# Six-step F(3,3) groups beside F(2,3) groups in a dilated convolution with a tanh-sigmoid gate

## The chip, the cores and the metric

The kernel runs on one core of a Trainium2 chip. The metric is the device time of one execution in microseconds (us). The profile is one execution of the program on the chip, taken by the hardware profiler. Its engines are called TensorE (PE in the rows, PEld for its weight loads), VectorE (DVE), ScalarE (ACT), GpSimd (POOL) and SyncE (SP, the queue from which most DMAs are issued).

## What is computed

Two sequences of 16000 steps with 256 channels (bf16) go through a causal convolution with three taps and dilation 2, to 512 channels. The first 256 channels pass through tanh, the other 256 through a sigmoid, the two are multiplied, and the product is multiplied by a 256x256 matrix.

```python
B, T, D, K = (2, 16000, 256, 3)
xp = jnp.pad(x, ((0, 0), (4, 0), (0, 0)))
h = jnp.einsum('btc,cd->btd', xp[:, 4:4 + T, :], w[0])
for i in range(1, K):
    off = 4 - 2 * i
    h = h + jnp.einsum('btc,cd->btd', xp[:, off:off + T, :], w[i])
f, g = h[..., :D], h[..., D:]
out = (jnp.tanh(f) * sigmoid(g)) @ w_o
```

So h[t] = x[t] w0 + x[t-2] w1 + x[t-4] w2. Steps of one parity form a chain of their own, and a short-filter (Winograd) scheme can be used on it: F(2,3) makes two successive outputs of a chain from four products instead of six, F(3,3) three from five instead of nine. The price is sums: of inputs and of weights ahead of the products, and of products behind them.

## The kernel before, in words

**Tiling.** The steps are cut into rows of four. A group is 256 rows (1024 steps; the first and the last group have 160), and a column of a matmul is one row and one parity, 512 columns in all. A transposed DMA (`load_chunk`, L115) brings x with channels on partitions; two groups share a load. For each group VectorE makes the sums `mm` (L185) and `pp` (L191), and GpSimd the four pieces of the differences `dd` (L202). A piece on GpSimd is made to wait for the VectorE instruction named `last`, so that it runs while VectorE's combine reads PSUM.

**Blocks.** A group has four blocks, one for each 128 of the 512 output channels, and the main loop runs over blocks `k`. A block has four products of two matmuls each (`products`, L226). Product 2 goes into bank `b`, ScalarE copies it (`ss`, L257), product 1 is added to `b`, VectorE makes `a = -2 ss + b` (L265), and products 0 and 3 are added to `b` and `a`. ScalarE then applies tanh or sigmoid to both banks (L281). In slot `k` of the loop TensorE does product 2 of block k, product 1 of block k-1, products 0 and 3 of block k-2, and one output piece.

**Output.** `gate` (L290) multiplies tanh and sigmoid halves. `out_mm` (L301) multiplies 128 rows and two steps by `w_o`, `out_evict` (L315) has ScalarE copy the piece to `osb`, and a DMA on SP stores it (L318). A 256-row group has four pieces.

**Start.** The first group (160 rows) is brought in plainly, transposed on TensorE and computed directly with nine products' worth of matmuls (`direct`, L246), while VectorE makes the weight sums `wm` and `wp` (L151 to L154). `direct` accumulates into bank `a` behind a VectorE memset (L243).

All work is issued by hand in program order (a manual schedule): each engine takes its instructions in that order, and waits come from the data and from buffers that must come free (three each of the banks `a` and `b`, two for output pieces).

Of the kernel before, what the change touches and what calls it, by code (L numbers as in the profile page):

```python
# [13 lines left out]
def kernel(  # L14
# [10 lines left out]

# [12 lines left out]
    P = 128  # L38
# [8 lines left out]
    FIRST = (160,)  # L47
    TILES = ((0, 80), (80, 80))
    N_DIRECT = 4

    def sizes(first):
        rem, rs = T // 4, []
        for r in first:
            r = min(r, rem)
            if r > 0:
                rs.append(r)
                rem -= r
        while rem > 0:
            rs.append(min(RG, rem))
            rem -= rs[-1]  # L60
        return rs


    groups, chunks = [], []
    for b in range(B):
        r0 = 0
        rs = sizes(FIRST if b == 0 else ())
        cuts = [1, 1] if b == 0 else []
        i = 0
        while i < len(rs):  # L70
# [33 lines left out]
    xts = {}  # L104

    def load_chunk(c):
        b, r0, rc, _, _ = chunks[c]
        xt = xt_pool.tile([P, 4, CT, RH + XW], bf16, name="xt")
        xts[c] = xt
        if r0 == 0:  # L110
            nc.gpsimd.memset(xt[:, :, :, RH - 1:RH], 0.0)
        if c == 0:
            return
        lo = 0 if r0 == 0 else RH
        nc.sync.dma_start_transpose(  # L115
            out=xt[:, :, :, RH - lo:RH + rc].rearrange("p j ct r -> p (j ct) r"),
            in_=x[b, 4 * (r0 - lo):4 * (r0 + rc), :].rearrange("(r j) c -> r (j c)", j=4),
        )

# [18 lines left out]
    nc.sync.dma_start(out=wo_sb[:], in_=w_o.rearrange("(ct c) d -> c ct d", c=P))  # L138
    ident = consts.tile([P, P], bf16)
    make_identity(nc, ident[:])  # L140
    for c in range(3):
        load_chunk(c)
    loaded = 3

    wh_sb = consts.tile([P, CT, D2], bf16)
    wt_sb = consts.tile([P, CT, D2], f32)
    wp_sb = consts.tile([P, CT, D2], bf16)
    wm_sb = consts.tile([P, CT, D2], bf16)

    def weights():  # L150
        nc.vector.tensor_scalar_mul(wh_sb[:], w_taps[1], 0.5)  # L151
        nc.vector.tensor_tensor(out=wt_sb[:], in0=w_taps[0][:], in1=w_taps[2], op=ALU.add)  # L152
        for dst, op in ((wm_sb, ALU.subtract), (wp_sb, ALU.add)):
            nc.vector.scalar_tensor_tensor(  # L154
                out=dst[:], in0=wt_sb[:], scalar=0.5, in1=wh_sb[:], op0=ALU.mult, op1=op,
            )

    def turn(i):
        r0, r = TILES[i]
        for h in range(2):  # L160
# [8 lines left out]
            dst = xts[0][:, 2 * h:2 * h + 2, :, RH + r0:RH + r0 + r]  # L169
# [5 lines left out]
    def views(g):  # L175
        G = groups[g]
        xt, c, R = xts[G["chunk"]], RH + G["col"], G["R"]
        return (xt[:, 0:2, :, c - 1:c - 1 + R], xt[:, 2:4, :, c - 1:c - 1 + R],
                xt[:, 0:2, :, c:c + R], xt[:, 2:4, :, c:c + R])

    def pre_m(g):
        xp, yp, xc, yc = views(g)
        G = groups[g]
        G["m"] = m_pool.tile([P, 2, CT, RG], bf16, name="mm")
        return nc.vector.tensor_tensor(out=G["m"][:, :, :, :G["R"]], in0=xc, in1=yp, op=ALU.subtract)  # L185

    def pre_p(g):
        xp, yp, xc, yc = views(g)
        G = groups[g]
        G["p"] = p_pool.tile([P, 2, CT, RG], bf16, name="pp")  # L190
        return nc.vector.tensor_tensor(out=G["p"][:, :, :, :G["R"]], in0=xc, in1=yp, op=ALU.add)  # L191

    def pre_d(g, part, eng, behind=None):
        xp, yp, xc, yc = views(g)
        G = groups[g]
        R = G["R"]
        if "d" not in G:
            G["d"] = d_pool.tile([P, 4, CT, RG], bf16, name="dd")
        h, q = divmod(part, 2)
        a, s = (yc, yp) if h == 0 else (xp, xc)  # L200
        j = 2 + q if h == 0 else q
        ins = eng.tensor_tensor(out=G["d"][:, j, :, :R], in0=a[:, q], in1=s[:, q], op=ALU.subtract)  # L202
        if behind is not None:
# [4 lines left out]
            )  # L208

    def products(k, which):  # L210
        g, oi = divmod(k, 4)
        G = groups[g]
        o = O_ORDER[oi]
        osl = slice(o * P, (o + 1) * P)
        R = G["R"]
        N = 2 * R
        if which == 2:
            G["b", oi] = ps_b.tile([P, 2 * RG], f32, name="b")
        wmat, mv, bank, first = {
            2: (wm_sb, lambda ct: G["m"][:, :, ct, :R], "b", True),  # L220
            1: (wp_sb, lambda ct: G["p"][:, :, ct, :R], "b", False),
            0: (w_taps[2], lambda ct: G["d"][:, 0:2, ct, :R], "b", False),
            3: (w_taps[0], lambda ct: G["d"][:, 2:4, ct, :R], "a", False),
        }[which]
        for ct in range(CT):
            nc.tensor.matmul(  # L226
                G[bank, oi][:, :N], lhsT=wmat[:, ct, osl], rhs=mv(ct),
                start=first and ct == 0, stop=ct == CT - 1, skip_group_check=True,
            )

    def direct(k, taps):

        g, oi = divmod(k, 4)
        G = groups[g]
# [3 lines left out]
        xp, yp, xc, yc = views(g)  # L238
        for tap in taps:
            if tap == 0:  # L240
                G["a", oi] = ps_a.tile([P, 2 * RG], f32, name="a")
                G["b", oi] = ps_b.tile([P, 2 * RG], f32, name="b")
                nc.vector.memset(G["a", oi][:, :2 * R], 0.0)  # L243
            for bank, mv in (("b", (xc, yp, xp)[tap]), ("a", (yc, xc, yp)[tap])):
                for ct in range(CT):
                    nc.tensor.matmul(  # L246
                        G[bank, oi][:, :2 * R], lhsT=w_taps[tap][:, ct, osl], rhs=mv[:, :, ct, :],
                        start=bank == "b" and tap == 0 and ct == 0, stop=tap == K - 1 and ct == CT - 1,
# [3 lines left out]
    def copy_m2(k):  # L252
        g, oi = divmod(k, 4)
        G = groups[g]
        N = 2 * G["R"]
        G["ss", oi] = ss_pool.tile([P, 2 * RG], f32, name="ss")
        nc.scalar.copy(out=G["ss", oi][:, :N], in_=G["b", oi][:, :N])  # L257

    def combine(k):

        g, oi = divmod(k, 4)
        G = groups[g]
        N = 2 * G["R"]
        G["a", oi] = ps_a.tile([P, 2 * RG], f32, name="a")
        nc.vector.scalar_tensor_tensor(  # L265
            out=G["a", oi][:, :N], in0=G["ss", oi][:, :N], scalar=-2.0, in1=G["b", oi][:, :N],
            op0=ALU.mult, op1=ALU.add,
        )

    def activate(k):  # L270
        g, oi = divmod(k, 4)
        G = groups[g]
        R = G["R"]
        o = O_ORDER[oi]
        if oi == 0:
            G["th"] = act_pool.tile([P, NT, 4, RG], bf16, name="th")
            G["sg"] = act_pool.tile([P, NT, 4, RG], bf16, name="sg")
            G["z"] = z_pool.tile([P, NT, 4, RG], bf16, name="zz")
        dst = G["th"][:, o] if o < NT else G["sg"][:, o - NT]
        for h, bank in ((0, "b"), (1, "a")):  # L280
            nc.scalar.activation(  # L281
                out=dst[:, 2 * h:2 * h + 2, :R],
                in_=G[bank, oi][:, :2 * R].rearrange("p (q r) -> p q r", q=2),
                func=ACT.Tanh if o < NT else ACT.Sigmoid,
            )

    def gate(g, dt):
        G = groups[g]
        R = G["R"]
        return nc.vector.tensor_tensor(  # L290
            out=G["z"][:, dt, :, :R], in0=G["th"][:, dt, :, :R], in1=G["sg"][:, dt, :, :R], op=ALU.mult
# [14 lines left out]
    def out_evict(g, rb0, jp, on_dve):  # L306
        G = groups[g]
        rn = min(P, G["R"] - rb0)
        if jp == 0:
            G["osb", rb0] = osb_pool.tile([P, 4, D], bf16, name="osb")  # L310
        osb, o_ps = G["osb", rb0], G["o", rb0, jp]
        if on_dve:
            nc.vector.tensor_copy(out=osb[:rn, 2 * jp:2 * jp + 2, :], in_=o_ps[:rn])
        else:
            nc.scalar.copy(out=osb[:rn, 2 * jp:2 * jp + 2, :], in_=o_ps[:rn])  # L315
        if jp == 1:
            t0 = 4 * (G["r0"] + rb0)
            nc.sync.dma_start(  # L318
                out=out[G["b"], t0:t0 + 4 * rn, :].rearrange("(p j) d -> p j d", j=4), in_=osb[:rn]
# [3 lines left out]
    NG = len(groups)  # L323
    NB = 4 * NG
    todo, made = [], []
# [3 lines left out]
    for tap in range(K):  # L329
        for k in range(2):  # L330
            direct(k, (tap,))
    weights()
    for k in range(2):
        activate(k)
    direct(2, range(K))
    activate(2)
    gate(0, 0)
    pre_m(1)
    pre_p(1)
    for part in range(3):  # L340
        last = pre_d(1, part, nc.vector)
    pre_d(1, 3, nc.gpsimd, last)

    direct(3, range(K - 1))
    products(N_DIRECT, 2)
    copy_m2(N_DIRECT)
    direct(3, (K - 1,))
# [79 lines left out]
```

## Time and profile before

| | |
|---|---|
| median of 3 runs | 292.33 us (292.31 to 292.58) |
| the profiled execution | 291.31 us |
| its span, first to last instruction | 289.4 us |
| granted TensorE clock | 1.00 |
| TensorE busy | 280.0 us, 1577 matmuls |
| ScalarE busy | 260.0 us, 511 instructions |
| VectorE busy | 198.2 us, 265 instructions |
| GpSimd busy | 127.0 us, 129 instructions |
| transposed loads, stores | 16, 64 |

Records of one engine overlap a little, since an instruction starts while the one before it drains. So the time that one costs when an engine is full is the distance of two starts, not the record's duration. In a row of the timeline stand start, duration, engine, line, operation, output tile and input tiles, shape and count; in brackets, how long the engine was idle before it and who released it. In a row of a group stand busy time and mean duration in ns, and the idle time ahead.

### The profile page before, as it was taken

To read this page: it belongs to the slowest core of one execution; us is meant where nothing else is said; L and a number is where in the kernel's file an instruction comes from. 1 tells how busy PE (TensorE), PEld (TensorE's weight loads), DVE (VectorE), ACT (ScalarE), POOL (GpSimd) and SP (SyncE) were. 2 spreads that over 40 slices of the span, in tenths; PEclk is the share of its full clock that TensorE was granted. 3 is DMA by queue.
4 is the path that set the end of the run, shared out by engine and by line. 5 is a ranking of instruction groups with operands and counts; after the bars stand their busy time and mean duration, and the time that the engine had idled before them with its cause. 6 is when DMAs were issued, how large, how long until landed. Compare 5 with 4: busy or idle time off the path is not lost.

```text
span 289.4 us, 4582 instructions
## 1 busy us (share of the span) xinstructions
PE 280.0 (97%) x1577; PEld 152.9 (53%) x1577; DVE 198.2 (68%) x265; ACT 260.0 (90%) x511; POOL 127.0 (44%) x129
## 2 busy tenths in 40 slices
PE   7689999999999999999999999999999999999994
PEld 3444555555555555555555555555555555555573
DVE  2966677677677677677677677677677677676540
ACT  2359999999999999999999999999999999999995
POOL 1264454454454454454454454454454454454200
PEclk9999999999999999999999999999999999999999
DMA  7960854272814709163281815519263261211213
GB/s 206 193 152 36 194 143 120 76 183 75 202 56 120 179 36 218 74 151 110 76 187 70 192 74 138 154 47 213 75 161 97 79 170 57 76 57 52 75 72 118
DMA packets 75462, 34.46 MB, mean 119 GB/s; under 512 B 66256, under 2 KB 67280, under 8 KB 75440
## 3 DMA queue, kind: packets, MB, share of 16 engines
q1 hardware_dynamic: 74640, 33.40, 43.2%
q10 hardware_dynamic: 800, 0.79, 0.9%
q8 instruction: 12, 0.20, 0.3%
q14 instruction: 10, 0.08, 0.1%
HBM read 1.25 MB, written 16.38 MB: 61 GB/s over the span
## 4 chain that ended last, share of the span: by engine, by line
PE 91%; DVE 3%; ACT 3%; DMA 2%; issue 0%; ACTq 0%
PE b L226 54%; PE o_ps L301 18%; PE a L226 18%; DMA w_sb<-in_w_dram 2%; ACT osb L315 1%; ACT th L281 1%; DVE wm_sb L154 0%; DVE wt_sb L152 0%; DVE wp_sb L154 0%; ACT sg L281 0%; DVE dd L202 0%; PE a L246 0%; DVE zz L290 0%; ACT ss L257 0%; DVE a L243 0%
## 5 line engine op out<-in xcount | busy, mean ns | idle before, releaser
L202 POOL TENSOR_TENSOR dd<-xt 128x512 bf16<-128x512 bf16 (+1 forms) x121 | 126.1, 1043 | 144.7 <-DVE zz L290 94.2
L265 DVE SCALAR_TENSOR_TENSOR a<-ss,b 128x512 f32<-128x512 f32 (+1 forms) x124 | 85.5, 690 | 31.0 <-PE b L226 30.0
L226 PEld LDWEIGHTS <-w_sb 128*128 128x128 bf16 x496 | 48.5, 98 | 57.1 <-DVE a L265 0.4
L257 ACT COPY ss<-b 128x512 f32<-128x512 f32 (+1 forms) x124 | 75.6, 610 | 3.2 <-PE b L226 3.1
L290 DVE TENSOR_TENSOR zz<-th,sg 128x1024 bf16<-128x1024 bf16 (+1 forms) x64 | 43.9, 686 | 48.8 <-ACT sg L281 48.8
L301 PE MATMUL o_ps<-wo_sb,zz 128*128 128x256 bf16 (+1 forms) x512 | 76.4, 273 | 0.6 <-ACT osb L315 0.6
L315 ACT CAST osb<-o_ps 128x512 bf16<-128x512 f32 (+1 forms) x128 | 75.4, 592 | 0.5 <-ACT osb L315 0.5
L226 PE MATMUL b<-mm,wm_sb 128*128 128x512 bf16 (+1 forms) x248 | 73.1, 376 | 0.3 <-ACT th L281 0.3
L226 PE MATMUL b<-dd,w_sb 128*128 128x512 bf16 (+1 forms) x248 | 73.1, 376 | 0.0
L226 PE MATMUL a<-dd,w_sb 128*128 128x512 bf16 (+1 forms) x248 | 73.1, 376 | 0.0
L226 PE MATMUL b<-pp,wp_sb 128*128 128x512 bf16 (+1 forms) x248 | 73.1, 376 | 0.0
L301 PEld LDWEIGHTS <-zz 128*128 128x128 bf16 (+1 forms) x512 | 49.9, 98 | 32.9 <-issue 1.3
L281 ACT ACTIVATE th<-b 128x512 bf16<-128x512 f32 (+1 forms) x64 | 37.6, 588 | 12.1 <-PE b L246 5.1
L281 ACT ACTIVATE sg<-b 128x512 bf16<-128x512 f32 (+1 forms) x64 | 37.6, 587 | 6.8 <-PE b L226 0.6
L226 PEld LDWEIGHTS <-wp_sb 128*128 128x128 bf16 x248 | 24.3, 98 | 28.5 <-issue 0.3
L185 DVE TENSOR_TENSOR mm<-xt 128x1024 bf16<-128x1024 bf16 (+1 forms) x32 | 37.9, 1185 | 0.0
L281 ACT ACTIVATE th<-a 128x512 bf16<-128x512 f32 (+1 forms) x64 | 37.2, 582 | 0.0
L281 ACT ACTIVATE sg<-a 128x512 bf16<-128x512 f32 (+1 forms) x64 | 37.2, 582 | 0.0
L191 DVE TENSOR_TENSOR pp<-xt 128x1024 bf16<-128x1024 bf16 (+1 forms) x31 | 34.3, 1106 | 0.0
L226 PEld LDWEIGHTS <-wm_sb 128*128 128x128 bf16 x248 | 24.1, 98 | 4.2 <-issue 1.0
L246 PE MATMUL a<-xt,w_sb 128*128 128x320 bf16 x24 | 5.2, 299 | 3.1 <-DVE a L243 3.1
L246 PEld LDWEIGHTS <-w_sb 128*128 128x128 bf16 x48 | 4.6, 97 | 5.8 <-DVE a L243 2.0
(22 smaller groups left out, 22.3 us busy)
## 6 DMA issues: line engine op xcount, KB each, us to landing
out_dram<-osb SPq DMA_DIRECT2D x62, 256.0 KB, 2.0
w_sb<-in_w_dram ACTq DMA_DIRECT2D x1, 512.0 KB, 5.8
xn<-in_x_dram SPq DMA_DIRECT2D x2, 160.0 KB, 3.7
w_sb<-in_w_dram ACTq DMA_DIRECT2D x1, 256.0 KB, 3.9
xt<-in_x_dram SPq DMA_TRANSPOSE x16, 6.6
wo_sb<-in_w_o_dram SPq DMA_DIRECT2D x1, 128.0 KB, 5.6
out_dram<-osb SPq DMA_DIRECT2D x2, 64.0 KB, 1.6
```

Of the source, the lines that this page charges most:

```text
L185: return nc.vector.tensor_tensor(out=G["m"][:, :, :, :G["R"]], in0=xc, in1=yp, op=ALU.subtract)
L191: return nc.vector.tensor_tensor(out=G["p"][:, :, :, :G["R"]], in0=xc, in1=yp, op=ALU.add)
L202: ins = eng.tensor_tensor(out=G["d"][:, j, :, :R], in0=a[:, q], in1=s[:, q], op=ALU.subtract)
L226: nc.tensor.matmul(G[bank, oi][:, :N], lhsT=wmat[:, ct, osl], rhs=mv(ct), start=first and ct == 0, stop=ct == CT - 1, skip_group_check=True,)
L246: nc.tensor.matmul(G[bank, oi][:, :2 * R], lhsT=w_taps[tap][:, ct, osl], rhs=mv[:, :, ct, :], start=bank == "b" and tap == 0 and ct == 0, ...
L257: nc.scalar.copy(out=G["ss", oi][:, :N], in_=G["b", oi][:, :N])
L265: nc.vector.scalar_tensor_tensor(out=G["a", oi][:, :N], in0=G["ss", oi][:, :N], scalar=-2.0, in1=G["b", oi][:, :N], op0=ALU.mult, op1=ALU.add,
L281: nc.scalar.activation(out=dst[:, 2 * h:2 * h + 2, :R], in_=G[bank, oi][:, :2 * R].rearrange("p (q r) -> p q r", q=2), func=ACT.Tanh if o ...
L290: return nc.vector.tensor_tensor(out=G["z"][:, dt, :, :R], in0=G["th"][:, dt, :, :R], in1=G["sg"][:, dt, :, :R], op=ALU.mult)
L301: nc.tensor.matmul(o_ps[:rn, q, :], lhsT=G["z"][:, dt, 2 * jp + q, rb0:rb0 + rn], rhs=wo_sb[:, dt, :], start=(dt == 0), stop=(dt == NT - 1),)
L315: nc.scalar.copy(out=osb[:rn, 2 * jp:2 * jp + 2, :], in_=o_ps[:rn])
```

## The change

The steps are cut anew. Beside the groups of four-step rows (kind B, F(2,3) as before) there are groups of six-step rows (kind A, F(3,3), 256 rows, 1536 steps). There are ten A groups: four in the first sequence, six in the second; 15 full B groups, one B group of 160 rows at the end, and the direct group (P) at the start. The blocks run in a written order: four B groups alone, then ten times a B group and an A group interleaved block by block, then the last two B groups alone.

An A block has five products: `first` (weights `wa` = w2/6 + w1/3 + 2 w0/3, operand `u1`), `mid` (`wm`, `rm`), `last` (`wp`, `rp`), `zero` (w2, `r0`) and `inf` (w0, `ri`). ScalarE copies `first` to `ss` before `mid` is added to the bank. VectorE then makes `halfway` (`hh = 1.5 ss - b`, into SBUF), and after `last` both `a = 3 ss + b` and `y = 2 hh + b` (into SBUF). The three outputs are activated from `b`, `y` and `a`.

The operands of an A group are made by VectorE (`u1, e, uh, rm, u0, u2, ud, f, rp`, spread over eight slots one pair ahead) and GpSimd (`r0`, `ri` in four pieces). The first A group's are all made by VectorE. B operands of the paired groups are made eight slots ahead.

Further: a B and an A load are separate, one per group; the first product's weights `wu` are scaled by ScalarE at the start, `wu` and `wa` are finished by VectorE between the first slots; `direct` has no memsets, starts bank `a` with the start flag and takes it from the output pieces' two buffers; `w_o` is loaded after the first transposed load. The order on TensorE within a slot depends on the kinds (`PE_ORDER`), a B slot may take two output pieces, and a block's `a` is activated one slot later, at that slot's start.

```diff
-    xt_pool = ctx.enter_context(tc.tile_pool(name="xt", bufs=3))
...
+    ROWS = {"P": 4, "B": 4, "A": 6}
+    LEAD = 4
+    N_SWAP = (2, 0)
...
+        n = (T - t) // (10 * RG) - N_SWAP[b]
+        for _ in range(n):
+            t = group("A", b, group("B", b, t, RG), RG)
+        while T - t > 0:
+            t = group("B", b, t, min(RG, (T - t) // 4))
+    As, Bs = of_kind["A"], of_kind["B"]
+    last = LEAD + len(As)
+    seq = [(g, oi) for g in Bs[:LEAD] for oi in range(4)]
+    for i, g in enumerate(Bs[LEAD:last]):
+        seq += [(h, oi) for oi in range(4) for h in (g, As[i])]
+    seq += [(g, oi) for g in Bs[last:] for oi in range(4)]
...
+    loads = sorted(As + Bs, key=lambda g: begin[g] - (6 if g in As else 0))
...
+    xt_pool = ctx.enter_context(tc.tile_pool(name="xt", bufs=4))
...
+            "u0": lambda: (ALU.subtract, None, cur[0], prev[1]),
+            "u1": lambda: (ALU.subtract, None, cur[1], prev[2]),
+            "u2": lambda: (ALU.subtract, None, cur[2], cur[0]),
+            "e": lambda: (ALU.subtract, None, cur[0], prev[2]),
+            "f": lambda: (ALU.add, None, cur[0], prev[2]),
+            "rp": lambda: (ALU.subtract, None, v("f"), v("u1")),
+            "rm": lambda: (ALU.add, -1.0 / 3.0, v("u1"), v("e")),
+            "uh": lambda: (None, 0.5, v("u1"), None),
+            "ud": lambda: (None, 2.0, v("u1"), None),
+            "r0": lambda: (ALU.subtract, None, v("uh"), v("u0")),
+            "ri": lambda: (ALU.subtract, None, v("u2"), v("ud")),
...
+            "A": {"first": (wa_sb, "u1", "b"), "mid": (wm_sb, "rm", "b"), "last": (wp_sb, "rp", "b"),
+                  "zero": (w_taps[2], "r0", "b"), "inf": (w_taps[0], "ri", "a")},
+            "B": {"first": (wm_sb, "m", "b"), "last": (wp_sb, "p", "b"),
+                  "zero": (w_taps[2], "d0", "b"), "inf": (w_taps[0], "d3", "a")},
...
-                G["a", oi] = ps_a.tile([P, 2 * RG], f32, name="a")
                 G["b", oi] = ps_b.tile([P, 2 * RG], f32, name="b")
-                nc.vector.memset(G["a", oi][:, :2 * R], 0.0)
+                G["a", oi] = ps_o.tile([P, 2 * RG], f32, name="a0", tag="o_ps")
...
+    def halfway(blk):
...
+        stt(G["hh", oi][:, :n], G["ss", oi][:, :n], 1.5, G["b", oi][:, :n], ALU.subtract)
...
+        stt(G["a", oi][:, :n], ss, 3.0 if G["kind"] == "A" else -2.0, b)
+        if G["kind"] == "A":
+            G["y", oi] = ss_pool.tile([P, 2 * RG], f32, name="yy")
+            stt(G["y", oi][:, :n], G["hh", oi][:, :n], 2.0, b)
...
+    for d, what in enumerate((
+        "m0 p0", "d00", "d30", "m1 wu", "p1 wa", "d01 u1", "d31 e", "m2", "p2 rm", "d02", "d32 u0",
+        "m3", "p3 r0v", "d03", "d33 u2", "m4", "p4 riv", "d04 f", "d34 rp",
+    ), -1):
...
+    for i, g in enumerate(Bs):
+        s = begin[g]
+        ahead = 8 if LEAD < i < last else 4
+        if i > LEAD:
+            plan(at_v, g, s - ahead, "m")
+            plan(at_v, g, s - min(3, ahead - 1), "p")
+        if i > LEAD:
+            for n, what in enumerate(("d3.0", "d3.1", "d0.0", "d0.1")):
+                plan(at_p, g, s - ahead + n, what)
+    for g in As[1:]:
+        s = begin[g] - 1
+        for d, what in ((-8, "u1"), (-7, "e"), (-6, "uh"), (-5, "rm u0"), (-4, "u2 ud"), (-2, "f"), (-1, "rp")):
+            plan(at_v, g, s + d, what)
+        for d, what in ((-4, "r0.0"), (-3, "r0.1"), (-2, "ri.0"), (-1, "ri.1")):
+            plan(at_p, g, s + d, what)
...
+    PE_ORDER = {"A": "FLZIM12", "B": "FZLI12", "BB": "FZLI12", None: "LZI12"}
...
+        n = 2 if not b0 or (kind == "B" and len(todo) >= 6) else 1
...
+        if b3:
+            activate(b3, "a")
+        for piece in made[:1]:
+            out_evict(*piece)
...
+        done = prepare(at_v, k, nc.vector)
+        if b3 and b3[1] in (1, 3):
+            g, dt = b3[0], b3[1] // 2
+            done = gate(g, dt)
...
+        prepare(at_p, k, nc.gpsimd, done)
+        if b1:
+            combine(b1)
+        if b0 and kind == "A":
+            halfway(b0)
+
+        while loaded < len(loads) and begin[loads[loaded]] <= k + 17:
+            load(loads[loaded])
             loaded += 1
         k += 1
```

In the loop of slots `b0`, `b1`, `b2`, `b3` are the blocks of this slot and of the three before it. The letters of `PE_ORDER` stand for the products first (F) and mid (M) of b0, last (L) of b1, zero (Z) and inf (I) of b2, and the output pieces (1, 2).

More of the change, by code (lines that the diff above doesn't have):

```diff
@@ L176, in views @@
         G = groups[g]
[L177 to L191, printed above, removed]
@@ L208, in pre_d, with product @@
             )
-    def products(k, which):
-        g, oi = divmod(k, 4)
+        return ins
+    def product(blk, which):
+        g, oi = blk
         G = groups[g]
@@ L256, in copy_m2 @@
         G["ss", oi] = ss_pool.tile([P, 2 * RG], f32, name="ss")
[L257 to L285 removed]
+        nc.scalar.copy(out=G["ss", oi][:, :n], in_=G["b", oi][:, :n])
@@ L329 @@
     for tap in range(K):
[L330 to L334, printed above, removed]
+        for oi in range(2):
+            direct(oi, (tap,))
+    nc.scalar.mul(wu_sb[:], w_taps[1], 1.0 / 3.0)
+    wb = weights_b()
+    next(wb)
+    for oi in range(2):
+        activate((0, oi), "b")
+        activate((0, oi), "a")
     direct(2, range(K))
-    activate(2)
+    activate((0, 2), "b")
+    activate((0, 2), "a")
+    next(wb)
+    prepare(at_v, -1, nc.vector)
```

330 lines of the change are left out of this document (189 added, 141 removed).

## The prediction

> **What bounds the kernel now.** I read the page's busy sums first, then its chain, then the timeline of a steady stretch, engine by engine, and last the first 27 us.
>
> ```profile
> span 289.4 us, 4582 instructions
> PE 280.0 (97%) x1577; PEld 152.9 (53%) x1577; DVE 198.2 (68%) x265; ACT 260.0 (90%) x511; POOL 127.0 (44%) x129
> PE 91%; DVE 3%; ACT 3%; DMA 2%; issue 0%; ACTq 0%
> ```
>
> The chain of waits is TensorE for 91% of the span: matmul time is what the end waits for. VectorE has a third of the span free, ScalarE a tenth. The profiled execution took 291.31 us, 1.9 more than its span and 1.02 less than the median of 292.33; I make the sum against 291.31 and add 1.02 at the end. Changes below 0.2% (0.6 us) I count as none.
>
> The timeline of one steady block on TensorE (start, duration; two 512-column matmuls a row, four 256-column ones for the output):
>
> ```profile
> 150.16 0.59 PE L226 MATMUL b<-mm,wm_sb 128*128 128x512 bf16 x2
> 150.60 0.59 PE L226 MATMUL b<-pp,wp_sb 128*128 128x512 bf16 x2
> 151.03 0.59 PE L226 MATMUL b<-dd,w_sb 128*128 128x512 bf16 x2
> 151.46 0.59 PE L226 MATMUL a<-dd,w_sb 128*128 128x512 bf16 x2
> 151.89 0.60 PE L301 MATMUL o_ps<-wo_sb,zz 128*128 128x256 bf16 x4
> 152.33 0.59 PE L226 MATMUL b<-mm,wm_sb 128*128 128x512 bf16 x2
> ```
>
> Rows overlap, so starts are what counts: 0.434 us for one product (two matmuls) and 0.434 for one output piece, 2.17 for the block, no gap.
>
> **The matmuls.** Before: 30 full groups x 4 blocks x 4 products = 480. After: 15 full B groups give 240, ten A groups 10 x 4 x 5 = 200; the 160-row groups and the 128 output pieces stay. 40 products fewer x 0.434 = **-17.4 us**, if TensorE goes on without gaps. An A group and its B group (a "pair", 2560 outputs) then take 36 products and 10 pieces, 46 x 0.434 = 19.96 us, where the same outputs took 10 x 2.17 = 21.7. The other engines must fit into 19.96.
>
> **VectorE.** Its rows, the undisturbed ones early in the run:
>
> ```profile
> 7.08 0.43 DVE L151 TENSOR_SCALAR wh_sb<-w_sb 128x1024 bf16<-128x1024 bf16 x1 [0.32 <-DMA w_sb<-in_w_dram]
> 7.43 1.22 DVE L152 TENSOR_TENSOR wt_sb<-w_sb 128x1024 f32<-128x1024 bf16 x1
> 8.68 1.22 DVE L154 SCALAR_TENSOR_TENSOR wm_sb<-wt_sb,wh_sb 128x1024 bf16<-128x1024 f32 x1
> 9.82 1.22 DVE L154 SCALAR_TENSOR_TENSOR wp_sb<-wt_sb,wh_sb 128x1024 bf16<-128x1024 f32 x1
> 12.21 0.68 DVE L185 TENSOR_TENSOR mm<-xt 128x1024 bf16<-128x1024 bf16 x1
> 12.81 0.68 DVE L191 TENSOR_TENSOR pp<-xt 128x1024 bf16<-128x1024 bf16 x1
> 152.78 0.69 DVE L290 TENSOR_TENSOR zz<-th,sg 128x1024 bf16<-128x1024 bf16 x1 [0.78 <-ACT sg L281]
> 153.39 0.70 DVE L265 SCALAR_TENSOR_TENSOR a<-ss,b 128x512 f32<-128x512 f32 x1
> 154.00 1.29 DVE L185 TENSOR_TENSOR mm<-xt 128x1024 bf16<-128x1024 bf16 x1
> 153.70 1.04 POOL L202 TENSOR_TENSOR dd<-xt 128x512 bf16<-128x512 bf16 x1 [1.76 <-DVE zz L290]
> 157.10 0.69 DVE L290 TENSOR_TENSOR zz<-th,sg 128x1024 bf16<-128x1024 bf16 x1 [0.78 <-ACT sg L281]
> 157.88 1.04 POOL L202 TENSOR_TENSOR dd<-xt 128x512 bf16<-128x512 bf16 x1 [1.46 <-DVE zz L290]
> L185 DVE TENSOR_TENSOR mm<-xt 128x1024 bf16<-128x1024 bf16 x31 | 37.1, 1200 | 0.0
> L191 DVE TENSOR_TENSOR pp<-xt 128x1024 bf16<-128x1024 bf16 x30 | 33.7, 1122 | 0.0
> ```
>
> From start to start: a 1024-column sum or a B gate 0.605, a PSUM combine 0.605 (153.39 to 154.00), a scaling 0.35 (7.08 to 7.43), a three-operand 1024-column sum 1.14 (8.68 to 9.82), an A gate of 1536 columns 0.605 x 1.5 = 0.9, an estimate. A pair has 16 combines (A: two and a halfway per block, B: one) 9.7; u1, e, u0, u2, f, rp, m, p 4.8; rm 1.1; uh and ud 0.7; two B gates 1.2 and two A gates 1.8: **19.4 us, 97% of TensorE's 19.96.** Before it was about 14 in 21.7. The spare time is gone, so order decides.
>
> The rows from 152.78 on carry the danger. The sum mm, 0.68 alone, took 1.29 beside a GpSimd subtraction and ended (155.29) 0.55 after that one's end (154.74): it stood still until then. The combine before it, one operand in SBUF and one in PSUM, kept its 0.70. In the new order each slot issues its sums, the GpSimd piece (1.04, as now) is released by the last of them, and two combines (1.21) follow, so the next sum, whose data phase begins 0.13 after its start (0.68 - 0.55), wants the memory 1.21 + 0.13 - 0.08 = 1.26 after that release (0.08: rows overlap by so much); GpSimd starts 0.09 (157.79 to 157.88) to 0.23 (153.47 to 153.70) after its releaser and ends 1.13 to 1.27 after it. I take 0 for this stall; its upper end is the row's 0.6 at each of 8 sums.
>
> No row has a combine that writes SBUF (halfway, y). Ends: 0.605 like `a`, or stopped by GpSimd like mm. I take 0.605, because `a` is the nearest row. [...]
>
> **The order within a pair.** I number its slots 0 to 7 (B first) and walk them with those prices. TensorE's slots: 2.17 (B, one piece), 2.60 (B with two pieces, slots 4 and 6; A). What a combine waits for:
>
> ```profile
> 151.30 0.69 DVE L265 SCALAR_TENSOR_TENSOR a<-ss,b 128x512 f32<-128x512 f32 x1 [0.48 <-PE b L226]
> ```
>
> It starts 0.70 after its product's start (150.60). VectorE's demand by slot: 2.4, 2.4, 2.5, 2.9 (rm and u0), 2.2, 2.4, 2.7, 1.8. Start at slot 0 behind a halfway that itself waits for TensorE. Slots 0 to 2: the second A combine ends 2.06 after the product "last" starts, and product "zero" of two slots on (2.17 later) needs it: fits by 0.1. Slot 3 is 0.3 too long: its halfway ends 1.23 into slot 4, where "last" wants to go 0.87 in. TensorE stands for **0.36**. Slot 4 is short, slot 5's halfway waits for TensorE again (0.3 spare), slot 6's excess ends in slot 7's 0.7. Nine pairs prepare a successor: 9 x 0.36 = **+3.2 us**. Ends: 0, and 1.0 a pair (rows 0.1 longer in slots 0 to 4), 10.
>
> **ScalarE.** Rows of one block:
>
> ```profile
> 149.50 0.60 ACT L281 ACTIVATE th<-b 128x512 bf16<-128x512 f32 x1
> 149.99 0.59 ACT L281 ACTIVATE th<-a 128x512 bf16<-128x512 f32 x1
> 150.47 0.59 ACT L315 CAST osb<-o_ps 128x512 bf16<-128x512 f32 x1
> 150.93 0.62 ACT L257 COPY ss<-b 128x512 f32<-128x512 f32 x1
> 151.66 0.60 ACT L281 ACTIVATE sg<-b 128x512 bf16<-128x512 f32 x1
> ```
>
> 0.48 from start to start; the copy, whose successor waits for TensorE, between 0.48 and 0.73, taken as 0.57 since its record is hardly longer. An A block has a copy, three activations and 1.5 evictions, a B block a copy, two and one: 38 per pair, 38 x 0.48 + 8 x 0.09 = 19.0 of 19.96. Slot 7, with two evictions, hands 0.5 to the short slot 0, whose activation of b frees the bank of slot 1's first product some 0.15 late: 10 x 0.15 = **+1.5** (ends 0 and 3). The third activation reads SBUF, which no row here does; taken as 0.48. [...] The new product "mid" waits for the copy of its own block: the copy ends some 1.3 into the slot, mid wants to go at 1.73, so it costs nothing as long as ScalarE is less than 0.4 behind.
>
> **GpSimd and DMA.** GpSimd: 8 x 1.04 = 8.3 of 19.96, no bound. SP's queue: transposed loads 26 instead of 16, in order with the stores.
>
> ```profile
> 1.65 0.42 SPq L138 DMA_DIRECT2D wo_sb<-in_w_o_dram  x1
> 2.12 4.78 SPq L115 DMA_TRANSPOSE xt<-in_x_dram  x1
> 6.94 4.59 SPq L115 DMA_TRANSPOSE xt<-in_x_dram  x1
> 30.15 4.02 SPq L115 DMA_TRANSPOSE xt<-in_x_dram  x1
> DMA to landing us min/median/max: 5.9/6.6/8.1
> ```
>
> A load holds SP some 4 to 4.8 us (30.15 is a 512-row one, so a 256-row six-step one should do likewise): 9 a pair, issued 16 slots (40 us) ahead of a need 8 slots before use. Hidden; a store behind two loads goes 9 us later, covered by three osb buffers, except at the very end, where no loads are left.
>
> **The head.**
>
> ```profile
> 9.59 0.43 PE L246 MATMUL b<-xt,w_sb 128*128 128x320 bf16 x2
> 11.48 0.43 PE L246 MATMUL a<-xt,w_sb 128*128 128x320 bf16 x2 [1.46 <-DVE a L243]
> 14.96 0.44 PE L246 MATMUL a<-xt,w_sb 128*128 128x320 bf16 x2 [1.67 <-DVE a L243]
> 15.78 0.59 PE L226 MATMUL b<-mm,wm_sb 128*128 128x512 bf16 x2
> 22.11 0.59 PE L226 MATMUL b<-mm,wm_sb 128*128 128x512 bf16 x2
> ```
>
> The direct group waited 3.1 us for memsets queued behind VectorE's weight sums; the memsets go (start flags instead). A direct product is 0.27 (three from 14.96 to 15.78); the last of blocks 0 and 1 starts at 9.59, ten more come before the first B product, which can start near 12.6 instead of 15.78. It doesn't stay so: wu and wa (1.14 each) on VectorE in slots 2 and 3 hold combines 0 to 2 back by about 1.1 in all, and block 4 starts near 20.0 instead of 22.11, with one output piece (0.43) more done: -2.5. But As[0]'s load is fourth on SP: 1.7 + 4.8 + 0.4 + 4.6 + 4.6 = 16.1, landing at 22.7, and its u1 stands in VectorE's order at about 21.2, ahead of a combine: 1.5 lost. Net **-1.0** (ends -3 and +1). ScalarE's new scaling into wu hides ahead of its first activation. The tail is the same two B groups: 0.
>
> **Sum.** 291.31 - 17.4 + 3.2 + 1.5 - 1.0 = 277.6; + 1.02 = **278.6 us**.
>
> **Rivals.**
> 1. Clean overlap: no gap in the pairs: 291.31 - 17.4 - 1 + 1 = 274, with the head at its best 272. For it: 0.6 us a pair free on VectorE. Against: slots 3 and 7. Chance 0.08.
> 2. [...] Chance 0.17.
> 3. Slower: the standstill of mm recurs at each of a pair's eight two-SBUF-input sums, because GpSimd's piece, released late by a gate, still runs when the next slot's sum starts. 8 x 0.5 = 4.0: VectorE's pair 23.4, 10 x (23.4 - 21.7) = +17, less the head: about **308**. It decides from 21.7 a pair, 0.3 us a slot over my 19.4. For it: before, nearly every mm and pp has just this stall. Against: there only one combine stood between release and sum, now two. Chance 0.16.
> 4. No change: TensorE's saving is eaten exactly (21.7 a pair). 0.02.
> My forecast: 0.57.
>
> Range: 272 to 289, which leaves out rivals 3 and 4. The forecast's own range, with the ends of its terms that don't add up to a rival, is 274 to 283. Faster 0.82, same 0.02, slower 0.16.
>
> **What would show it.** TensorE's starts within a pair 0.434 apart except a gap ahead of "last" in slot 4 released by VectorE; a pair near 20.5 us; sums (u1, e, m, p) near 0.7 each; busy VectorE near 95% in the paired stretch; the first wm product near 12.6; u1's first instance waiting for DMA. Sums near 1.2 with TensorE waiting for VectorE in every slot would make me wrong, as would ScalarE's activations ending TensorE's gaps.

## The result, and the profile after

The changed kernel takes **281.32 us** (median of 4, 280.9 to 281.75) against 292.32: 0.9625 of the time before, with a 95% interval from 0.9606 to 0.9644. The forecast was 278.6 us with a range from 272 to 289: the direction and the range held, and the gain is 11.0 us instead of 13.7.

Page of the changed kernel: span and instructions, busy time of each engine, the chain's shares.

```profile
span 279.7 us, 4411 instructions
PE 270.2 (97%) x1497; PEld 145.1 (52%) x1497; DVE 240.6 (86%) x379; ACT 249.6 (89%) x492; POOL 86.8 (31%) x88
PE 82%; DVE 12%; ACT 2%; DMA 2%; issue 1%; SPq 0%; DVEq 0%; ACTq 0%
```

TensorE has 80 matmuls less. VectorE went from 198 to 241 us busy in a shorter span, and it now holds 12% of the chain instead of 3%: it is the second limit.

The prices of the new VectorE work, and of ScalarE's, by groups (busy time, mean ns):

```profile
L289 DVE SCALAR_TENSOR_TENSOR hh<-ss,b 128x512 f32<-128x512 f32 x40 | 27.3, 682 | 8.5 <-PE b L258 7.3 <-ACT sg L321 0.6 <-ACT th L321 0.6
L289 DVE SCALAR_TENSOR_TENSOR yy<-hh,b 128x512 f32<-128x512 f32 x40 | 27.1, 679 | 0.0
L229 DVE TENSOR_TENSOR m<-xt 128x1024 bf16<-128x1024 bf16 x15 | 10.3, 690 | 0.0
L229 DVE TENSOR_TENSOR p<-xt 128x1024 bf16<-128x1024 bf16 x15 | 10.9, 725 | 0.0
L332 DVE TENSOR_TENSOR zz<-th,sg 128x1536 bf16<-128x1536 bf16 x20 | 19.0, 951 | 0.6 <-ACT sg L321 0.5
L321 ACT ACTIVATE sg<-yy 128x512 bf16<-128x512 f32 x20 | 13.5, 673 | 0.3 <-DVE yy L289 0.3
L321 ACT ACTIVATE sg<-b 128x512 bf16<-128x512 f32 x50 | 31.2, 624 | 1.0 <-PE b L258 1.0
```

The combines hh and yy cost what `a` costs (0.69), and the sums m and p are down to 0.69 and 0.73 from the 1.20 and 1.12 of mm and pp: GpSimd hardly stops them any more.

The loop's slots 0 to 15 are the four leading B groups, pair 1 begins at slot 16, and slot 96 is the first behind the ten pairs. The stretches of pairs 1, 2, 3, 4 and 10 (start and end, length, then busy time with instructions of TensorE, its weight loads, VectorE, ScalarE and GpSimd, granted clock, DMA share and GB/s):

```profile
47.88:68.86 20.98, 19.54 (x102) 9.74 (x100) 20.84 (x34) 18.08 (x36) 8.29 (x8) 1.00 0.46 119
68.86:89.33 20.47, 19.80 (x102) 9.59 (x101) 19.62 (x32) 18.10 (x35) 9.17 (x9) 1.00 0.50 96
89.33:109.57 20.24, 20.23 (x114) 10.86 (x112) 19.49 (x32) 18.91 (x38) 8.87 (x9) 1.00 0.60 135
109.57:129.82 20.25, 20.24 (x115) 10.87 (x113) 19.50 (x32) 19.22 (x39) 8.85 (x9) 1.00 0.52 133
231.05:250.96 19.91, 19.91 (x114) 10.96 (x112) 14.64 (x23) 19.16 (x39) 4.12 (x4) 1.00 0.17 67
```

A steady pair has VectorE busy for 19.50 us, as worked out (19.4). The last pair, which prepares no successor, takes 19.91, TensorE's own time. Pairs 1 and 2 have twelve matmuls (three output pieces) less than the others and still take longer. This is where a part of the gain went.

Slot 4 of a steady pair on TensorE:

```profile
119.10 0.59 PE L258 MATMUL b<-m,wm_sb 128*128 128x512 bf16 x2
119.70 0.59 PE L258 MATMUL b<-d,w_sb 128*128 128x512 bf16 x2
120.29 0.59 PE L258 MATMUL b<-rp,wp_sb 128*128 128x512 bf16 x2
120.72 0.59 PE L258 MATMUL a<-d,w_sb 128*128 128x512 bf16 x2
```

Two steps are 0.60 and 0.59 instead of 0.43: TensorE stands for 0.17 ahead of "zero" and for 0.16 ahead of "last". These are the only gaps of over 0.05 in a steady pair.

The end, from the start of the last full group, before and after (columns as above). After the change it has six output pieces more (21 instead of 15):

```profile
264.82:289.43 24.61, 20.64 (x136) 12.94 (x133) 9.95 (x17) 20.89 (x45) 2.88 (x4) 1.00 0.22 82
250.96:279.66 28.70, 24.14 (x160) 15.18 (x157) 11.22 (x19) 24.90 (x53) 2.84 (x4) 0.99 0.27 104
```

The sum of the spans, forecast against measured. A product or a piece is counted at 0.4327, the mean of the 100 blocks of before from 48.49 to 264.82; what a stretch takes beyond that is its gap.

| term | forecast | measured |
|---|---|---|
| 40 products | -17.4 | -17.3 |
| up to slot 16 (before 48.49, after 47.88) | -1.0 | -0.6 |
| pairs 3 to 9, slot 4 | +2.5 | 7 x (20.25 - 46 x 0.4327) = +2.4 |
| pairs 1 and 2 | +0.7 | 41.45 - 2 x 43 x 0.4327 = +4.2 |
| ScalarE, slot 1 | +1.5 | 0 |
| from the last full group's start to the end | 0 | 28.70 - 24.61 - 6 pieces x 0.4327 = +1.5 |
| sum | -13.7 | -9.8 (279.7 - 289.4 = -9.7) |

### The profile page after: what moved, and what is told of

It reads as the page before. It is cut to its first block, busy times and chain, and to the rows that moved or that the text cites. A ratio compares the mean times of both kernels' runs of the same rounds, so it can differ in the third digit from the quotient of the medians.

```text
span 279.7 us, 4411 instructions
## 1 busy us (share of the span) xinstructions
PE 270.2 (97%) x1497; PEld 145.1 (52%) x1497; DVE 240.6 (86%) x379; ACT 249.6 (89%) x492; POOL 86.8 (31%) x88
## 4 chain that ended last, share of the span: by engine, by line
PE 82%; DVE 12%; ACT 2%; DMA 2%; issue 1%; SPq 0%; DVEq 0%; ACTq 0%
PE b L258 48%; PE o_ps L343 18%; PE a L258 13%; DVE a L289 3%; DVE zz L332 2%; DMA xn<-in_x_dram 2%; DVE yy L289 1%; DVE hh L289 1%; PE b L275 1%; PE a L275 1%; ACT osb L355 1%; DVE u L229 1%; DVE d L229 1%; DVE f L229 1%; ACT sg L321 1%
## 5 line engine op out<-in xcount | busy, mean ns | idle before, releaser
L229 POOL TENSOR_TENSOR d<-xt 128x512 bf16<-128x512 bf16 (+1 forms) x44 | 44.4, 1010 | 127.2 <-DVE zz L332 78.7
L332 DVE TENSOR_TENSOR zz<-th,sg 128x1024 bf16<-128x1024 bf16 (+2 forms) x54 | 41.5, 768 | 7.6 <-ACT sg L321 7.4
L258 PE MATMUL b<-d,w_sb 128*128 128x512 bf16 (+1 forms) x128 | 37.4, 373 | 2.0 <-DVE a L289 1.9
L258 PE MATMUL b<-m,wm_sb 128*128 128x512 bf16 (+1 forms) x128 | 37.4, 374 | 0.0
L258 PE MATMUL a<-d,w_sb 128*128 128x512 bf16 (+1 forms) x128 | 37.4, 374 | 0.0
L258 PE MATMUL b<-p,wp_sb 128*128 128x512 bf16 (+1 forms) x128 | 37.4, 374 | 0.0
L321 ACT ACTIVATE th<-a 128x512 bf16<-128x512 f32 (+1 forms) x54 | 32.5, 603 | 3.5 <-PE a L258 2.1
L289 DVE SCALAR_TENSOR_TENSOR hh<-ss,b 128x512 f32<-128x512 f32 x40 | 27.3, 682 | 8.5 <-PE b L258 7.3
L258 PEld LDWEIGHTS <-wp_sb 128*128 128x128 bf16 x208 | 20.2, 97 | 26.0 <-issue 3.3
L229 POOL TENSOR_TENSOR ri<-u,ud 128x512 bf16<-128x512 bf16 x18 | 20.8, 1155 | 22.3 <-DVE zz L332 16.7
L229 POOL TENSOR_TENSOR r<-uh,u 128x512 bf16<-128x512 bf16 x18 | 20.8, 1156 | 21.6 <-DVE zz L332 11.1
L289 DVE SCALAR_TENSOR_TENSOR yy<-hh,b 128x512 f32<-128x512 f32 x40 | 27.1, 679 | 0.0
L258 PEld LDWEIGHTS <-wm_sb 128*128 128x128 bf16 x208 | 20.2, 98 | 12.4 <-issue 0.6
```

The lines of the kernel that those rows point to most:

```text
L229: ins = eng.tensor_tensor(out=o, in0=a[:, qs], in1=b[:, qs], op=op)
L258: nc.tensor.matmul(G[bank, oi][:, :2 * R], lhsT=wmat[:, ct, osl], rhs=G[mv][:, :, ct, :R], start=which == "first" and ct == 0, stop=ct == ...
L289: return nc.vector.scalar_tensor_tensor(out=out, in0=in0, scalar=scalar, in1=in1, op0=ALU.mult, op1=op)
L321: nc.scalar.activation(out=G[name, dt][:, j:j + 2, :R], in_=G[bank, oi][:, :2 * R].rearrange("p (q r) -> p q r", q=2), func=(ACT.Tanh, ACT ...
L332: return nc.vector.tensor_tensor(out=G["z"][:, dt, :, :R], in0=G["th", dt][:, :, :R], in1=G["sg", dt][:, :, :R], op=ALU.mult)
```

## The experiments

All times are medians on one core, each beside runs of the kernel before, whose median lay between 291.6 and 292.3 us. The last two runs were made on another chip than the other experiments. Slots 0 to 7 are those of a pair, as in the prediction; slots from 16 on are counted by the loop.

**The gap in slot 4.** Theory: slot 3 asks too much of VectorE. Rival: VectorE's whole demand is the limit. The edit moves u0 from slot 3 to slot 4, and u2 and f to later slots.

```diff
-        for d, what in ((-8, "u1"), (-7, "e"), (-6, "uh"), (-5, "rm u0"), (-4, "u2 ud"), (-2, "f"), (-1, "rp")):
+        for d, what in ((-8, "u1"), (-7, "e"), (-6, "uh"), (-5, "rm"), (-4, "u0 ud"), (-2, "u2"), (-1, "f rp")):
```

> The sums of an A group's operands are moved by a slot: u0 from slot 3 to 4, u2 from 4 to 6, f from 6 to 7, nothing else. Theory (slot 3 of a pair asks 0.3 us too much of VectorE, its halfway comes late and TensorE stands 0.17 ahead of zero and 0.16 ahead of last in slot 4): both gaps go, a steady pair takes 19.9 to 20.0 instead of 20.25, and the kernel 278.6 us (8 x 0.33 less). Rival (VectorE's whole demand of 19.5 a pair is the bound, the place doesn't matter): the gap comes back in slots 6 to 0, a pair stays at 20.2, the kernel at 281.0 to 281.6.

Measured: 277.65 us (277.31 to 279.66), 0.9528 of before (0.9501 to 0.9555). Slot 4 on TensorE:

```profile
116.84 0.59 PE L258 MATMUL b<-m,wm_sb 128*128 128x512 bf16 x2
117.27 0.59 PE L258 MATMUL b<-d,w_sb 128*128 128x512 bf16 x2
117.71 0.59 PE L258 MATMUL b<-rp,wp_sb 128*128 128x512 bf16 x2
```

The whole pair, in the columns of the stretches above, with the same work on VectorE:

```profile
107.24:127.23 19.99, 19.99 (x114) 10.86 (x112) 19.50 (x32) 19.20 (x39) 8.85 (x10) 1.00 0.51 135
```

The steps are 0.43 and 0.44, a pair takes 19.99 instead of 20.25, VectorE is busy for 19.50 as before. The place was the cause, not the amount. In the profiled executions the span fell by 3.8. The pairs make 2.1 of it, a little under the 2.6 of the theory, and 1.8 is a quicker start (below), not this edit.

**GpSimd's wait.** Theory: the wait keeps GpSimd and the two-input sums apart. Rival: they don't disturb each other.

```diff
-        prepare(at_p, k, nc.gpsimd, done)
+        prepare(at_p, k, nc.gpsimd, None)
```

> GpSimd's pieces no longer wait for the slot's last VectorE sum or gate, only for their data and buffers. Theory (a VectorE sum with two SBUF inputs stands still while GpSimd reads SBUF, and the wait is what keeps them apart): many sums take 1.0 to 1.3 us instead of 0.69, VectorE's demand rises by 2 to 4 us a pair over TensorE's 19.9, and the kernel takes 290 to 310 us; the combines, hh and yy among them, stay at 0.68. Rival (the two engines don't disturb each other here): sums stay at 0.69 and the kernel at 281, within 0.6.

Measured: **308.58 us** (307.51 to 309.92). One pair's slots 4 to 6 on VectorE:

```profile
129.69 1.37 DVE L227 TENSOR_SCALAR ud<-u 128x1024 bf16<-128x1024 bf16 x1
130.98 0.68 DVE L289 SCALAR_TENSOR_TENSOR a<-ss,b 128x512 f32<-128x512 f32 x1
131.58 0.68 DVE L289 SCALAR_TENSOR_TENSOR yy<-hh,b 128x512 f32<-128x512 f32 x1
132.86 1.64 DVE L332 TENSOR_TENSOR zz<-th,sg 128x1024 bf16<-128x1024 bf16 x1
135.02 0.67 DVE L289 SCALAR_TENSOR_TENSOR hh<-ss,b 128x512 f32<-128x512 f32 x1
135.62 1.33 DVE L229 TENSOR_TENSOR f<-xt 128x1024 bf16<-128x1024 bf16 x1
```

GpSimd beside them:

```profile
128.06 2.72 POOL L229 TENSOR_TENSOR r<-uh,u 128x512 bf16<-128x512 bf16 x2 [11.72 <-DVE u L229]
131.23 2.72 POOL L229 TENSOR_TENSOR ri<-u,ud 128x512 bf16<-128x512 bf16 x2 [0.45 <-DVE ud L227]
133.91 5.64 POOL L229 TENSOR_TENSOR d<-xt 128x512 bf16<-128x512 bf16 x4
```

With GpSimd's pieces in a row, a gate takes 1.64 instead of 0.68, f 1.33 instead of 0.69, ud 1.37 instead of 0.42; a, yy and hh beside them stay at 0.67 to 0.68. A pair takes 23.2. So the standstill that the slower rival feared is real, and the wait is worth 27 us. That the two combines behind the wait are needed as well was not tested. The 308.6 us meet the rival's 308 by chance: there the wait was to be in place and eight sums were to stand still for 0.5 each; here the wait is gone, and in this pair four instructions (ud, a B gate, f, and an A gate with 1.79 instead of 0.95) stand still for 0.6 to 1.0 each. So ud, which has a single input, stood still as well (1.37), and hh and yy, with one SBUF input, one PSUM input and an SBUF output, did not (0.67 and 0.68).

**Fewer pairs.** Theory: two pairs (40.5 us) stand in the place of five B groups, so each pair fewer costs half the difference. Rivals: the matmuls alone count, or pairs cost more than they show.

```diff
-    N_SWAP = (2, 0)
+    N_SWAP = (4, 0)
```

> Eight A groups instead of ten (two in the first sequence), five more B groups. Theory (a steady pair takes 20.25 and the five B groups that stand for two pairs 5 x 8.66 = 43.3): the kernel takes 2.8 us longer, 284.1. Rival (the matmuls count alone: 2 x 1.74): 3.5 longer, 284.8. Rival (pairs cost more than they show, by later pieces at the end): 282.5 or less.

Measured: 283.80 us (282.94 to 284.2), 2.5 more than with ten, 1.2 a pair. By the medians it lies between the theory's 284.1 and the last rival. They don't decide it, since the two kernels' starts differ (below): in the profiled executions the first B product stood at 13.89 here and at 14.33 with ten pairs, and from slot 16 to the end this kernel took 234.9 instead of 231.8, 3.1 more, halfway between the theory's 2.8 and the first rival's 3.5. What the run does show is that a steady pair takes 20.25 here too, and that fewer pairs are slower.

**The first pairs: missing pieces.** Theory: pairs 1 and 2 are set by VectorE, TensorE has too little to do there. Rival: late data.

```diff
-    z_pool = ctx.enter_context(tc.tile_pool(name="zz", bufs=2))
+    z_pool = ctx.enter_context(tc.tile_pool(name="zz", bufs=3))
...
+        if 6 <= k < 4 * LEAD and len(todo) <= 6:
+            n = 0
```

The gate's output gets a third buffer with it; what that does by itself was not tested.

> Six output pieces of the leading B groups are held back into the first pairs (and z gets a third buffer), so that pairs 1 and 2 have about ten pieces as the others instead of seven. Theory (pairs 1 and 2 are set by VectorE, since TensorE has only 18.6 us of work there against VectorE's 19.4 and more): the pieces fill TensorE's gaps, pairs 1 and 2 take no longer than before (20.98 and 20.47), the leading blocks lose up to 6 x 0.43 of TensorE's work but are near VectorE's pace too, so the kernel takes 279.5 to 281. Rival (the gaps of pairs 1 and 2 are late data, not missing pieces): the two pairs get 1.3 longer each and the kernel takes 281.3 to 283.

Measured: 279.14 us (278.85 to 281.54). Pairs 1 and 2:

```profile
47.52:69.16 21.64, 20.98 (x114) 10.92 (x112) 20.96 (x35) 19.32 (x38) 8.73 (x8) 1.00 0.47 125
69.16:89.18 20.02, 19.96 (x110) 10.43 (x108) 19.44 (x32) 18.93 (x38) 8.73 (x9) 1.00 0.57 123
```

With 10 and 9 pieces they took 21.64 and 20.02, together 41.66 against 41.45 with 7 and 7: five pieces (2.2 us of TensorE; the leading slots gave up five, not six) cost 0.2. The rival is out. The leading slots took 32.5 instead of 33.55. The two profiled executions have spans of 279.7 both, but this one started 0.7 later, so the edit gains 0.6. The rest of the 2.2 in the medians is put down to the start, which only the profiled execution shows.

**The first pair: two lists meet.** VectorE of the changed kernel in slots 16 and 17:

```profile
47.99 0.69 DVE L229 TENSOR_TENSOR d<-xt 128x1024 bf16<-128x1024 bf16 x1
48.59 0.69 DVE L229 TENSOR_TENSOR f<-xt 128x1024 bf16<-128x1024 bf16 x1
49.20 0.69 DVE L229 TENSOR_TENSOR m<-xt 128x1024 bf16<-128x1024 bf16 x1
49.80 0.69 DVE L229 TENSOR_TENSOR u<-xt 128x1024 bf16<-128x1024 bf16 x1
50.41 0.68 DVE L332 TENSOR_TENSOR zz<-th,sg 128x1024 bf16<-128x1024 bf16 x1
51.01 0.69 DVE L289 SCALAR_TENSOR_TENSOR a<-ss,b 128x512 f32<-128x512 f32 x1
51.61 1.22 DVE L229 TENSOR_TENSOR d<-xt 128x1024 bf16<-128x1024 bf16 x1
```

d and f come from the written list for the leading slots (positions 16 and 17), m and u1 from the plan for the next pair. The combine that "zero" waits for comes behind all of them. Theory: this meeting makes the two largest gaps of TensorE in pair 1, 0.85 and 0.78. Rival: GpSimd's first piece does (the 1.22 above).

```diff
-        "m0 p0", "d00", "d30", "m1 wu", "p1 wa", "d01 u1", "d31 e", "m2", "p2 rm", "d02", "d32 u0",
-        "m3", "p3 r0v", "d03", "d33 u2", "m4", "p4 riv", "d04 f", "d34 rp",
+        "m0 p0", "d00", "d30", "m1 wu", "p1 wa", "d01 u1", "d31 e", "m2", "p2 rm", "d02 f", "d32 u0",
+        "m3", "p3 r0v", "d03 rp", "d33 u2", "m4 d04", "p4 d34", "", "riv",
```

> In the list of the leading slots f, rp and the differences of the fifth B group come earlier (slots 8, 12, 14, 15), and only riv is left for slot 17. Theory (in slots 16 and 17 the end of that list meets the first pair's own plan, five sums and a gate in one slot, and makes the gaps of 0.85 and 0.78 us there): the two gaps shrink to about 0.3 each, the leading slots lose 0.2, and the kernel gains 0.7 to 1.2 us: 280.1 to 280.6 at the same start. Rival (the gaps come from GpSimd's first piece, which holds up a sum by 0.5 there): they go to about 0.5 and 0.8 and the kernel gains 0.3 or less.

Measured: 278.62 us (278.4 to 280.07). Pair 1:

```profile
47.91:67.50 19.59, 19.38 (x102) 9.75 (x100) 19.46 (x31) 18.08 (x36) 8.28 (x8) 1.00 0.52 128
```

It takes 19.59 instead of 20.98, the leading slots 33.85 instead of 33.55: 1.1 gained at a like start, as expected. The rest of the 2.7 in the medians is again put down to the start. The gaps became 0 and 0.25. In slot 17 the remaining riv still loses 0.53 to GpSimd's piece (1.75 instead of 1.22), so the rival's stall exists, but there is room for it.

**The start.** The first direct products on TensorE and what stands ahead of them, in the changed kernel and in the kernel with moved sums:

```profile
5.56 0.72 PE L168 MATMUL tp<-ident,xn 80*128 80x80 bf16 x8 [0.78 <-DMA xn<-in_x_dram]
6.08 1.48 PE L92 MATMUL a<-warm 128*128 128x512 bf16 x3
7.35 0.74 PE L275 MATMUL b<-xt,w_sb 128*128 128x320 bf16 x2
7.88 0.74 PE L275 MATMUL a<-xt,w_sb 128*128 128x320 bf16 x2
```

```profile
5.58 0.46 PE L168 MATMUL tp<-ident,xn 80*128 80x80 bf16 x8 [0.92 <-DMA xn<-in_x_dram]
5.88 0.81 PE L92 MATMUL a<-warm 128*128 128x512 bf16 x3
6.53 0.43 PE L275 MATMUL b<-xt,w_sb 128*128 128x320 bf16 x2
6.80 0.43 PE L275 MATMUL a<-xt,w_sb 128*128 128x320 bf16 x2
```

The program is the same up to there (before the direct products it runs transposes and `warm`, matmuls whose result nobody reads). One direct product takes 0.53 in the one execution and 0.27 in the other, a factor of two, and the first B product starts at 14.33 or at 12.54. Over the profiled executions of the runs with the same start it stood at 12.5, 13.0, 13.9, 13.9, 14.1, 14.3 and 15.0. The granted clock is 1.00 in all of them, so that column doesn't show it. Full pace was reached at places between 4 and 11 us: in the run without GpSimd's wait the first eight transposes, at 4.27, took 0.48 instead of 0.71, while in the run with held-back pieces the direct products still stepped by 0.53 up to 9.54. What turns the pace, no row shows; that TensorE had too little to do before is the theory of the next run.

```diff
-    N_WARM_A = 6
+    N_WARM_A = 8
...
     turn(0)
+    warm_up(2)
     turn(1)
```

> Eight instead of six warm-up matmuls at the start and two more between the two transposed tiles. Theory (in some executions TensorE still steps through its first direct products at half pace, 0.53 us for one instead of 0.27, because it had too little to do before; the first B product then starts at 14.3 to 15.0 instead of 12.5): every execution has the quick start, its first B product stands at 12.5 to 12.9, and the kernel takes 279.3 to 279.8 us, 1.5 to 2 less than the changed kernel. Rival (the slow start comes from where the direct products' data land): the first B product stays at 14.3 and the kernel at 281.3, or it is longer by the added matmuls, 282.

Measured: 280.31 us (280.0 to 280.56). The five times lie within 0.6, where the other kernels spread over 1.7 to 2.7 when both starts occur. The first B product stood at 13.24: the pace is full from the first direct product on (7.23, step 0.27), but the added matmuls hold the tiles' transposes back by about 0.5. So the gain was 1.0, not 1.5 to 2: the run agrees with the theory's cause, and nearly half of the gain went into the added matmuls. The narrow spread did not repeat: with the same warm-up the kernel of four edits (below) spread over 1.6.

**The end.** Theory: ScalarE's evictions of the six added pieces hold TensorE up. Rival: TensorE's own work and the two buffers set the end.

```diff
+        if on_dve:
+            nc.vector.tensor_copy(out=osb[:rn, 2 * jp:2 * jp + 2, :], in_=o_ps[:rn])
...
-                    out_evict(*piece)
+                    out_evict(*piece, k >= N - 4)
...
-                out_evict(*piece)
+                out_evict(*piece, True)
```

> In the last four slots and behind them, the second output piece of a slot is evicted by VectorE instead of ScalarE. Theory (the end has six pieces more than before the change and hangs on ScalarE's evictions, with 2.65 us of gaps on TensorE behind slot 96 against 1.13 before): the gaps fall to about 1.3 and the kernel takes 1.0 to 1.4 us less, 280.0 at the same start. Rival (TensorE's own work and the two buffers of the pieces set the end): no more than 0.4 less.

Measured: 280.74 us (279.14 to 281.63). The last pieces on TensorE, in the changed kernel and in this one:

```profile
270.48 0.60 PE L343 MATMUL o_ps<-wo_sb,zz 128*128 128x256 bf16 x4 [0.29 <-ACT osb L355]
272.41 0.60 PE L343 MATMUL o_ps<-wo_sb,zz 128*128 128x256 bf16 x4 [0.35 <-ACT osb L355]
273.23 1.09 PE L343 MATMUL o_ps<-wo_sb,zz 128*128 128x256 bf16 x8 [0.22 <-ACT osb L355]
274.50 1.87 PE L343 MATMUL o_ps<-wo_sb,zz 128*128 128x256 bf16 x12 [0.18 <-ACT osb L355]
```

```profile
271.82 1.88 PE L343 MATMUL o_ps<-wo_sb,zz 128*128 128x256 bf16 x12 [0.25 <-ACT osb L358]
273.93 1.14 PE L343 MATMUL o_ps<-wo_sb,zz 128*32 128x256 bf16 x8 [0.24 <-ACT osb L358]
```

Four stops for an eviction became two. TensorE's gaps behind slot 96 fell by 0.8, from 2.65 to 1.83, instead of the 1.0 to 1.4 expected, and the stretch from slot 96 to the end by 0.6, from 28.70 to 28.08. ScalarE's evictions are a part of the end's price. What the rest is (the two buffers, the last gate), this run doesn't take apart. The median's 0.6 is within the spread of the starts; the gaps and the stretch are the evidence.

**Together.** Moved sums, held-back pieces, the longer warm-up (8 and 2) and the evictions:

> The moved sums of the A operands, the held-back pieces, the longer warm-up and the evictions on VectorE at the end, together. If the four are independent: 281.3 - 2.1 - 0.7 - 1.7 - 1.2 = 275.6 us. If the held-back pieces and the moved sums work on the same gaps of pairs 1 and 2: 276 to 276.5.

Measured: 277.23 us (276.37 to 277.92). Pairs 3 and later take 20.0 to 20.2, but pair 1 takes 21.3 with its ten pieces: the two lists still meet there. The simple sum (275.6) counted 1.7 for the start and 1.2 for the end, where the single runs gave 1.0 and 0.6, and was 1.6 too low; the other expectation, 276 to 276.5, was too low as well.

With the earlier leading list in place of the held-back pieces, and a warm-up of 7 and 2:

> Four edits together, without the held-back pieces: the moved sums of the A operands, the earlier leading list, a warm-up of 7 matmuls and 2 between the tiles, evictions on VectorE at the end. If the leading list and the moved sums act on different gaps (slots 16 and 17 of the first pair; slot 4 of every pair), pair 1 takes 19.3, pairs 3 to 9 take 20.0, and the kernel 281.3 - 1.1 - 2.1 - 0.8 - 1.0 = 276.3 us. If they act on the same gaps, 277 or more.

Measured: **276.48 us** (275.66 to 276.99), 0.9467 of before (0.944 to 0.9493), the fastest of all, 4.8 us less than the changed kernel (4.6 by the ratios to the runs of before). Pair 1 took 19.24, pairs 4 to 9 20.0: the two edits work on different gaps.

The same with the held-back pieces (and the third buffer that goes with them):

> The same four edits, and six output pieces held back from the leading slots into pairs 1 and 2. If pairs 1 and 2, with the list out of the way, are still set by VectorE, the pieces cost nothing there and the leading slots get shorter: 0.5 to 1.0 less than without, 275.4 to 275.8. If TensorE sets them by then, the pieces only change place: within 0.3 of the kernel without.

Measured: 276.95 us (276.81 to 278.69). Pairs 1 and 2 took 20.25 and 19.92 instead of 19.24 and 20.33, while the leading slots took 33.97 instead of 33.86 with five pieces fewer. Both expectations were off by the medians, which differ by less than the times of either kernel among themselves. TensorE sets pair 1 by now (20.19 of 20.24 us busy), so the pieces cost time there, and the leading slots got no shorter without them. There VectorE is busy for 32.91 of 33.97 us, filled by the list; that this is why, no run shows by itself. Slot 96 begins at 246.69 here and at 246.60 without, though the first B product stood 0.84 earlier: the held-back pieces now lose about 0.9.

## Why the prediction came out as it did

**The limit and the matmuls: right.** TensorE stayed the chain, a product cost 0.433, and 40 of them were saved.

**VectorE's demand: right.** 19.50 us busy a pair against 19.4; the unknown combines hh and yy took 0.68 and lay at the lower of the two ends, and the A gate took 0.95, 0.87 from start to start (105.42 to 106.29), against the estimate of 0.9.

**The order within a pair: right in place and size.** The gap stands in slot 4, ahead of zero and last, 0.33 against 0.36, and goes when u0 leaves slot 3 (u2 and f moved with it).

**The standstill beside GpSimd: right.** It is at 0 in a steady pair but for 0.07 at p and rp. The prediction's reason is that two combines stand between release and next sum; the run without the wait shows that the standstill comes back (27 us), but not that two combines are needed.

**ScalarE, +1.5: wrong.** In a steady pair TensorE had no gap released by ScalarE. sg from yy took 0.67 and sg from b 0.62; on average over tanh and sigmoid an activation from yy (0.66) was some 0.04 longer than the others (0.62), and it cost nothing either. The range's upper end, 289, counted a higher price for that activation, which no run of before shows; the changed kernel showed these 0.04 and no gap of TensorE from them.

**The head, -1.0: -0.6 measured, out of two errors.** The first product without memset waits was put at 12.6 and stood at 12.54 where TensorE had its full pace; here it stood at 14.33, because of a start whose pace differs from execution to execution, which one trace of before (with the quick start) could not tell. And u1 was expected to wait 1.5 for the fourth load. It did not: five loads left SP in 15.1 us, 3.0 each instead of the 4.6 taken from two rows. That the two nearly cancelled is luck.

**The first pairs, and the end: the terms that failed.** "An A group and its B group then take 36 products and 10 pieces" was said for ten pairs. The first two have seven pieces, since the pieces of the first A group come only after it, and VectorE's 19.4 then exceeds TensorE's 18.6. In the first pair the list of the leading slots also meets the pair's own plan. Together their gaps took 4.2 instead of 0.7. The six pieces come at the end instead ("the tail is the same two B groups: 0"), where they cost 1.5 beyond their own time. ScalarE's evictions are a part of that (0.6 to 0.8); the rest stays open.

**How near the number came: in part luck.** The profiled execution was forecast at 277.6 and took 281.44, 3.8 more. The first pairs and the end cost 5.0 more than forecast and the head 0.4, while the 1.5 that ScalarE didn't need gave a part back. The 1.02 added for the median hid a further 1.0 of the miss, as the changed kernel's profiled execution lies on its median.

## What to carry to other kernels

When a change brings a second engine to 97% of the first, the order decides. Walk one period slot by slot with start-to-start distances from the trace, and then walk the first and the last period too: work that arrives a period late leaves the leading engine short at the start and has to be done at the end. Two engines, one of which makes the other stand still (a gate of 1.64 instead of 0.68 us), can be kept apart by one wait (308.58 us without it, 281.32 with it); here, work that isn't disturbed (a, hh and yy at 0.67 to 0.68 beside GpSimd's pieces) stands behind the release.

## What was not expected of the hardware

- The TensorE pace at the start: 0.53 or 0.27 us for one direct product in the same program, turning anywhere between 4 and 11 us (eight transposes at 4.27 in 0.48 in one run, direct products still 0.53 apart up to 9.54 in another), with a granted clock of 1.00 in the records throughout. Over the seven executions with the same start, the first B product moves by up to 2.5 us, which is more than most edits here gain.
- A single-input scaling on VectorE (ud) stood still beside GpSimd's pieces (1.37 instead of 0.42), like a sum with two inputs (f, 1.33 instead of 0.69).
- GpSimd's pieces r and ri (inputs from VectorE's own results) took 1.155 us, 18 of each; the 40 pieces d (inputs from the transposed tile) took 1.04 with the same shape and operation. Nothing here tells why.
